# Decode attention over a key/value cache: which eight heads of a batch share a tile

## The chip, the cores and the metric

The kernel runs on one core of one Trainium2 chip. The metric is the device time of one execution in microseconds (us). Besides the times of plain runs there is one profiled execution, from which all durations are taken: its trace holds every instruction with start and duration, and every packet that the core's 16 DMA engines moved, with start, duration and bytes.

## The reference

Four decode tokens (batch 4, one position each, width 640) go through a layer norm, and then through two branches that are added to the input:

```python
x = A_x                                    # (4, 1, 640) bf16
xn = _layernorm(x)
return x + _A_ref(xn, A_k_cache, A_v_cache, A_wq, A_wo) + _B_ref(xn, B_w_in, B_w_sp, B_b_sp, B_w_out)

def _A_ref(x, k_cache, v_cache, wq, wo):   # caches: (4, 32, 4096, 128) bf16, as many q heads as kv heads
    q = (x @ wq).reshape(B, 1, 32, 128).transpose(0, 2, 1, 3)
    scores = jnp.einsum('bhqd,bhkd->bhqk', q, k_cache) * 128 ** (-0.5)
    o = jnp.einsum('bhqk,bhkd->bhqd', _softmax(scores), v_cache)
    return o.transpose(0, 2, 1, 3).reshape(B, 1, 32 * 128) @ wo
```

`_B_ref` is a small gated MLP (a gMLP with one position) over weights of 640 x 1728 and 864 x 640. The caches are the bulk: K and V have 4 x 32 heads of 4096 rows of 128 values, 1 MiB per head, 134 MB each. wq and wo have 5.2 MB each.

## The kernel before, in words

**Tiles.** The 32 heads of a batch are cut into HG = 4 groups of HT = 8 heads. A tile i is one head group hg = i // 4 of one batch b = i % 4, so there are NT = 16 tiles for K and 16 for V. In a tile a head has LN = 16 of the 128 partitions, and a partition holds NC = 256 successive cache rows of its head, 64 KB. `run_view` (L113) gives the part of the cache that makes up a tile. Since the eight heads of a group follow each other in memory, the tile is 8 MiB without a gap, seen as 128 rows of 64 KB.

**Where tiles lie.** SBUF holds one ring of UNITS = 5 units; a unit is half a tile (128 x 32 KB). K tiles take two units (`load_k`, L134), V tiles mostly two in one load, at the start and the end one unit at a time, and the very last half in four cuts (`load_v`, L141, V_CUTS L132). wq comes first, into the units that K tile 1 takes later (L104 to L106). The gMLP weights go to one unit (`load_w`, L123). wo is loaded per head group (`load_wo`, L154): three times as 128 rows of 10 KB (L157), the last time in seven parts by head (L163).

**Order of the loads.** All of them are issued on SP's queue, in the order of the list that starts at L179: K tile 0, gMLP weights, K tile 1, V tile 0, wo of group 0, K tile 2, then V and K in turn. `pump` (L203) issues the next load of the list as soon as the work that last used its units has been recorded; on the chip SP then waits for the semaphores of that work. ACT's queue carries only x, two scalars and half of the output.

**Work.** The q projection (L338 to L347) multiplies the normed x with wq, in groups of QH = 4 heads (512 columns) by 5 slices of the width; `place`, `stage_q` (L499) and `q_lanes` spread a group's q over the partitions, so that each partition has the q of its head. Then for each tile, in four quarters: VectorE multiplies K with q (L525) and mostly adds the two halves of a head's width (L541), TensorE sums the products with the identity matrix (L550), VectorE finishes the row sums (L564). The maximum and the exponentials follow (L573 to L587), ScalarE deals the probabilities out to eight masked copies (L598), TensorE multiplies them with V (L623), and `gather` (L634) collects a tile's result. A group's four tiles are normalized, turned (`group_turn`, `group_pick`) and multiplied with the group's part of wo (`group_proj`, L717), which is added into one accumulator (`out_sum`) over all groups. That sum over the groups makes it immaterial which heads a group has, as long as the q columns and the wo rows are those of its heads. The order of the instructions on TensorE, VectorE, ScalarE and SP is that of the program (L732).

Of the kernel before, what the change touches and what calls it, by code (L numbers as in the profile page):

```python
# [20 lines left out]
def kernel(  # L21
# [14 lines left out]
    nc = tc.nc  # L36
    P = nc.NUM_PARTITIONS
    Bsz, Sq, D = A_x.shape
    _, H, S, Dh = A_k_cache.shape
    HD = A_wq.shape[1]  # L40
    F = B_w_in.shape[1]
    Fh = F // 2
    DC = D // P
# [4 lines left out]
    HT = 8  # L48
    HG = H // HT
    NT = HG * Bsz  # L50
    LN = P // HT
    NC = HT * S // P
# [7 lines left out]
    CG = P // CW  # L60
# [27 lines left out]
    def units(first, n=1):  # L88
        return ring[:, first * UNIT : (first + n) * UNIT]
# [6 lines left out]
    def pair(i):  # L96
        if i in (0, NT - 1):
            return 2 if i == 0 else V_PAIR
        return 1 if i % 2 == 0 else 0
# [2 lines left out]
        return (2, 3, 0, 1) if i == 0 or (i % 2 and i < NT - 1) else (0, 1, 2, 3)  # L102

    wq_flat = ring[:, pair(1) * UNIT : pair(1) * UNIT + DC * HD]  # L104
    wq_sb = wq_flat.rearrange("p (c n) -> p c n", n=HD)
    nc.sync.dma_start(out=wq_flat, in_=A_wq.rearrange("(p c) n -> p (c n)", c=DC))  # L106

    wsp_bf = const.tile([1, 1], BF16)
# [3 lines left out]

    def run_view(cache, i):  # L113
        hg, b = divmod(i, Bsz)
        return cache[b, HT * hg : HT * (hg + 1)].rearrange("h s d -> (h s) d").rearrange(
            "(p c) d -> p (c d)", c=NC
        )

    w_sb = units(W_UNIT)
    w_in_sb = w_sb[:, 0 : DC * F].rearrange("p (c n) -> p c n", c=DC)  # L120
# [13 lines left out]
    def load_k(i):  # L134
        t = units(pair(i), 2)
        step = (1 if i == 0 else 2) * UNIT
        for e in reversed(range(0, 2 * UNIT, step)):
            nc.sync.dma_start(out=t[:, e : e + step], in_=run_view(A_k_cache, i)[:, e : e + step])
        k_tiles[i] = t.rearrange("p (c d) -> p c d", d=Dh)

    def load_v(i, part, unit, n):  # L141
        t = units(unit, n)
        cuts = V_CUTS if (i, part) == (NT - 1, 1) else (0, n * UC)
        for c0, c1 in zip(cuts, cuts[1:]):
            src = slice((part * UC + c0) * Dh, (part * UC + c1) * Dh)
            nc.sync.dma_start(out=t[:, c0 * Dh : c1 * Dh], in_=run_view(A_v_cache, i)[:, src])
        for e in range(n):
            v_tiles[i, part + e] = units(unit + e).rearrange("p (c d) -> p c d", d=Dh)

    wo_r = A_wo.rearrange("(j p r) n -> j p (r n)", p=P, r=HT)  # L150
    wo_h = A_wo.rearrange("(j h p) n -> j p h n", p=P, h=HT)
    wo_tiles = {}

    def load_wo(j):  # L154
# [15 lines left out]
    def plan_k(i):  # L170
        plan(("k", i), pair(i), 2, load_k, i)

    def plan_v(i, part, unit, n=1):
        plan(("v", i, part), unit, n, load_v, i, part, unit, n)
# [28 lines left out]
    def pump():  # L203
        while loads:
# [29 lines left out]
        out=lane_diag[:],  # L234
        in_=ident_f[:].rearrange("p (h l) -> p l h", h=HT),
# [5 lines left out]
        out=hmask[:],  # L241
        in_=ident_f[:].rearrange("p (h l) -> p h l", h=HT),
# [5 lines left out]
        out=head_scale[:].rearrange("p (h l) -> p h l", h=HT),  # L248
# [11 lines left out]
        out=sel[:],  # L260
        in_=ident_f[:].rearrange("p (g h k) -> p k h g", g=CG, k=GC),
# [5 lines left out]
        out=spread[:],  # L267
        in_=ident[:].rearrange("p (m r) -> p r m", r=HT)[:, :, None, :].to_broadcast(
            [P, HT, HT, LN]
        ),  # L270
# [3 lines left out]
        out=q_lanes[:].rearrange("r b (h l) -> r b h l", h=HT),  # L274
        in_=ident[: HT * Bsz, : HT * Bsz]
# [4 lines left out]
    QW = CW  # L280
    QH = HT // 2
# [3 lines left out]
    for g in range(CG):  # L285
        ps = slice(g * QW, (g + 1) * QW)
        for hh in range(QH):
            at_col = (g % 2 * QH + hh) * Bsz
            nc.gpsimd.tensor_copy(
                out=place[ps, hh, at_col : at_col + Bsz], in_=lane_diag[ps, 0:Bsz]  # L290
# [12 lines left out]
    for i in range(NSTAT):  # L303
# [5 lines left out]
        out=rstd[:], in_=mv[:, 1:2], func=ACT.Sqrt, bias=eps_tile[:Bsz], scale=1.0  # L309
# [4 lines left out]
        out=xn_bf[:],  # L314
# [9 lines left out]
    for c in range(DC):  # L324
        nc.tensor.transpose(  # L325
            out=xnT_ps[:, c, :], in_=xn_v[:, c, :], identity=ident[:Bsz, :Bsz]
# [8 lines left out]
    q_ps = [  # L335
        ps_m.tile([P, QH * Dh], FP32, tag="m", name="q_ps") for _ in range(NQG // CG)
    ]
    for c in range(DC):  # L338
        for hg in range(NQG):
            g = hg % CG  # L340
            nc.tensor.matmul(  # L341
                out=q_ps[hg // CG][g * QW : (g + 1) * QW, :],
                lhsT=xnT[:, c, :],
                rhs=wq_sb[:, c, hg * QH * Dh : (hg + 1) * QH * Dh],
                start=(c == 0),
                stop=(c == DC - 1),
            )  # L347
# [6 lines left out]
    def out_sum(half):  # L354
        return out_ps[OG * half : OG * half + Bsz, :]

    for half in range(2):
        nc.tensor.matmul(
            out=out_sum(half),
            lhsT=ident[:Bsz, :Bsz],  # L360
            rhs=x_bf[:, half * NOH : (half + 1) * NOH],
# [486 lines left out]
```

## Time and profile before

| | |
|---|---|
| median of 3 runs | 662.41 us (662.41 to 662.49) |
| the profiled execution | 664.69 us |
| its span, first to last instruction | 662.9 us |
| VectorE (DVE) busy | 458.5 us, 69% |
| TensorE (PE) busy | 325.6 us, 49% |
| ScalarE (ACT) busy | 82.6 us, 12% |
| GpSimd (POOL) busy | 5.6 us, 1% |
| read from memory | 282.24 MB, 426 GB/s over the span |

How to read it: the busy time of an engine is the sum of its instructions; the engines run beside each other. The DMA engines are no compute engines: there are 16 of them, and the profile gives their mean busy share, as well as packets, bytes and share of each queue. q1 is SP's queue, q10 that of ACT. In a row of waits stand the engine and line that waited, what released it, the time in total, how often, and the longest. In a table of windows a row has the stretch, the busy time and number of instructions of PE, PE's weight loads, DVE, ACT and POOL, the granted TensorE clock, the DMA share and the rate in GB/s.

The packet records show what a load is made of: one packet for each contiguous row of a partition (64 KB for a whole K or V tile, 32 KB for a unit), and packets of 4 bytes, with which the engines that share a load report that they are done.

### The profile page before, as it was taken

What the parts mean: (1) busy time and instruction counts of PE and PEld (TensorE: products, weight loads), DVE (VectorE), ACT (ScalarE), POOL (GpSimd) and SP (SyncE); (2) the same over time, 40 slices, a digit from 0 to 9 for tenths busy, and PEclk for the clock granted to TensorE, in tenths of its full rate; (3) what the DMA queues carried; (4) which work ended last, traced back from release to release, by engine and by line L of the source; (5) the groups of instructions that cost most, each with busy time, mean ns of one, the idle gap of its engine ahead of it and who ended that gap; (6) DMA issues with size and microseconds to landing.
All of it is one profiled execution on the core that took longest, in us unless ns stands there. A gap on an engine that the chain in (4) does not pass through costs nothing.

```text
span 662.9 us, 4934 instructions
## 1 busy us (share of the span) xinstructions
PE 325.6 (49%) x2131; PEld 149.9 (23%) x2131; DVE 458.5 (69%) x265; ACT 82.6 (12%) x202; POOL 5.6 (1%) x29
## 2 busy tenths in 40 slices
PE   0356462635546263463526447253563526457746
PEld 0114130212212132131212223121231212213334
DVE  2495975939488594966949397692957949488940
ACT  0103102020200202011020200202020020200200
POOL 2000000000000000000000000000000000000000
PEclk9765685778877677585867877577786857867886
DMA  9999999999999999999999999999999999999997
GB/s 378 437 398 395 423 458 435 443 429 427 428 439 440 423 443 432 404 463 423 439 436 435 428 443 424 431 439 428 435 436 435 435 435 436 416 429 437 423 429 282
DMA packets 8049, 282.56 MB, mean 426 GB/s; under 512 B 880, under 2 KB 2140, under 8 KB 2524
## 3 DMA queue, kind: packets, MB, share of 16 engines
q1 hardware_dynamic: 8008, 282.25, 99.1%
q8 instruction: 16, 0.26, 0.1%
q14 instruction: 5, 0.04, 0.0%
q10 hardware_dynamic: 20, 0.01, 0.0%
HBM read 282.24 MB, written 0.01 MB: 426 GB/s over the span
## 4 chain that ended last, share of the span: by engine, by line
DMA 62%; DVE 26%; PE 11%; issue 0%; ACT 0%; DVEq 0%; ACTq 0%
DMA ring<-in_A_k_cache_dram 57%; DVE ring L525 19%; PE s_ps L550 8%; DVE ring L541 6%; DMA ring<-in_A_v_cache_dram 3%; DMA ring<-in_A_wq_dram 2%; PE q_ps L341 1%; PE pv_acc L623 1%; PE pv L641 0%; PE out_ps L721 0%; DVE s_sb L564 0%; PE pv L653 0%; ACT pv_sb L637 0%; DVE m L573 0%; ACT res L816 0%
## 5 line engine op out<-in xcount | busy, mean ns | idle before, releaser
L550 PE MATMUL s_ps<-ring,ident 128*128 128x512 bf16 x624 | 212.8, 507 | 291.8 <-DVE ring L541 159.8
L525 DVE TENSOR_TENSOR ring<-ring,qbc 128x8192 bf16<-128x8192 bf16 x64 | 281.8, 4418 | 97.9 <-DMA ring<-in_A_k_cache_dram 97.9
L550 PEld LDWEIGHTS <-ident 128*128 128x128 bf16 x624 | 75.8, 122 | 413.2 <-issue 286.1
L541 DVE TENSOR_TENSOR ring<-ring 128x4096 bf16<-128x4096 bf16 x50 | 114.6, 2291 | 1.6
L623 PE MATMUL pv_acc<-ring,pm 128*32 128x512 bf16 x1008 | 68.7, 412 | 7.3 <-DMA ring<-in_A_v_cache_dram 7.3
L564 DVE TENSOR_REDUCE s_sb<-s_ps 128x64 f32<-128x512 f32 x64 | 43.8, 685 | 25.3 <-PE s_ps L550 25.3
L637 ACT COPY pv_sb<-pv_acc 128x512 f32<-128x512 f32 x16 | 9.4, 586 | 397.5 <-PE pv_acc L623 397.5
L598 ACT ACTIVATE pm<-p,hmask 128x256 bf16<-128x256 bf16 x120 | 49.5, 494 | 0.5
L623 PEld LDWEIGHTS <-pm 128*32 128x32 bf16 x1008 | 38.3, 143 | 38.6 <-issue 28.5
L583 DVE TENSOR_REDUCE nb<-max_ps 128x1 f32<-128x16 f32 x16 | 2.8, 174 | 37.0 <-PE max_ps L577 37.0
L641 PE MATMUL pv<-sel,pv_sb 128*128 128x8 f32 x128 | 17.8, 265 | 11.1 <-ACT pv_sb L637 11.1
L641 PEld LDWEIGHTS pv<-sel,pv_sb 128*128 128x128 f32 x128 | 16.3, 199 | 18.3 <-ACT pv_sb L637 18.3
L682 DVE TENSOR_TENSOR o_n<-pv,rden 128x32 bf16<-128x32 f32 x4 | 0.8, 192 | 15.9 <-PE pv L653 15.8
L575 ACT ACTIVATE lay<-lane_diag,m 128x16 f32<-128x16 f32 x16 | 4.9, 309 | 47.6 <-DVE m L573 47.6
L587 ACT ACTIVATE p<-s_sb,nb 128x256 bf16<-128x256 f32 x16 | 8.1, 508 | 19.5 <-DVE nb L583 19.5
L577 PE MATMUL max_ps<-lay,head_scale 128*128 128x16 f32 x32 | 6.3, 272 | 3.7 <-ACT lay L575 3.7
L511 ACT CAST q_rows<-qr_ps 32x128 bf16<-32x128 f32 x4 | 1.0, 256 | 51.8 <-PE qr_ps L503 51.8
L665 POOL TENSOR_TENSOR own_sum<-acc,hmask 128x32 f32<-128x32 f32 x4 | 2.0, 500 | 621.1 <-ACT p L587 621.1
L573 DVE TENSOR_REDUCE m<-s_sb 128x1 f32<-128x256 f32 x16 | 6.7, 420 | 0.5
L341 PE MATMUL q_ps<-ring,xnT 128*32 128x512 bf16 x40 | 4.5, 631 | 3.9 <-DMA ring<-in_A_wq_dram 3.9
L577 PEld LDWEIGHTS max_ps<-lay,head_scale 128*128 128x128 f32 x32 | 5.0, 199 | 5.6 <-ACT lay L575 5.6
L325 PE MATMUL xnT_ps<-ident,xn_bf 4*128 4x4 bf16 x5 | 0.4, 178 | 11.5 <-DVE xn_bf L313 11.5
(90 smaller groups left out, 74.6 us busy)
## 6 DMA issues: line engine op xcount, KB each, us to landing
ring<-in_A_v_cache_dram SPq DMA_DIRECT2D x7, 4096.0 KB, 23.6
ring<-in_A_k_cache_dram SPq DMA_DIRECT2D x2, 4096.0 KB, 29.2
ring<-in_A_wq_dram SPq DMA_DIRECT2D x1, 5120.0 KB
wo<-in_A_wo_dram SPq DMA_DIRECT2D x3, 1280.0 KB, 25.9
ring<-in_B_w_in_dram SPq DMA_DIRECT2D x1, 2160.0 KB, 38.4
ring<-in_A_v_cache_dram SPq DMA_DIRECT2D x1, 2048.0 KB, 20.5
ring<-in_A_v_cache_dram SPq DMA_DIRECT2D x1, 1024.0 KB, 22.2
ring<-in_A_v_cache_dram SPq DMA_DIRECT2D x2, 512.0 KB
```

What stands on the lines that cost most here:

```text
L341: nc.tensor.matmul(out=q_ps[hg // CG][g * QW : (g + 1) * QW, :], lhsT=xnT[:, c, :], rhs=wq_sb[:, c, hg * QH * Dh : (hg + 1) * QH * Dh], st ...
L525: nc.vector.tensor_tensor(out=t, in0=t, in1=qbcs[i // Bsz][:, i % Bsz, None, :].to_broadcast([P, QC, Dh]), op=ALU.mult,)
L541: nc.vector.tensor_tensor(out=t[:, :, 0:HD2], in0=t[:, :, 0:HD2], in1=t[:, :, HD2:Dh], op=ALU.add)
L550: nc.tensor.matmul(out=s[:], lhsT=ident[:], rhs=t[:, :, g * RW : (g + 1) * RW], start=(g == 0), stop=(g == n - 1),)
L564: nc.vector.tensor_reduce(out=scores[i][:, q * QC : (q + 1) * QC], in_=sums_ps.pop((i, q))[:], axis=AX.X, op=ALU.add,)
L573: nc.vector.tensor_reduce(out=m1[:], in_=scores[i][:], axis=AX.X, op=ALU.max)
L577: nc.tensor.matmul(out=ps[:], lhsT=head_scale[:], rhs=d[:], start=True, stop=True)
L587: nc.scalar.activation(out=p[:], in_=scores.pop(i)[:], func=ACT.Exp, bias=nb[:], scale=scale_qk, accum_out=acc[hg % NACC][:, b : b + 1],)
L598: nc.scalar.activation(out=p_m[i % 2][:, :, h, :], in_=probs[i][:].rearrange("p (n c) -> p n c", c=BC), func=ACT.Copy, scale=hmask[:, h : ...
L623: nc.tensor.matmul(out=pv_acc[g * CW : (g + 1) * CW, :], lhsT=pm[:, n, :, :].rearrange("p h (k c) -> p c (h k)", k=GC)[:, c, :], rhs=v_nat ...
L637: nc.scalar.copy(out=pv_sb[:], in_=pv_acc[:])
L641: nc.tensor.matmul(out=pvs[hg][:, :, b], lhsT=pv_sb[:, k * Dh : (k + 1) * Dh], rhs=sel[:, k, :], start=(k == 0), stop=stop and k == GC - 1,)
```

## The change

A tile holds every fourth head of a batch (hg, hg + 4, ..., hg + 28) instead of eight neighbouring ones. The cache is viewed as `(h j) (l c) d -> j h l (c d)`, with j the group, h the head in it and l its 16 partitions, so that a tile is now 8 pieces of 1 MiB that lie 4 MiB apart; in the built instruction the source of a K or V load is [8 heads, 16 rows, run] and the destination 128 partitions with a run each. Before, it was [128 rows, run] on both sides. The wo rows follow: three of the four wo loads have such a source of 8 x 16 rows too, while the last group's wo, in parts by head, still has 128 rows. The wq load is as before; the q projection's matmuls take their 512 columns as four runs of 128. Everything else, and the order of the instructions on every engine, is unchanged. Lines move by two.

```diff
-    wq_sb = wq_flat.rearrange("p (c n) -> p c n", n=HD)
+    wq_heads = wq_flat.rearrange("p (c h j d) -> p c j h d", c=DC, h=HT, j=HG)
...
     def run_view(cache, i):
         hg, b = divmod(i, Bsz)
-        return cache[b, HT * hg : HT * (hg + 1)].rearrange("h s d -> (h s) d").rearrange(
-            "(p c) d -> p (c d)", c=NC
-        )
+        return cache[b].rearrange("(h j) (l c) d -> j h l (c d)", j=HG, c=NC)[hg]
...
-            nc.sync.dma_start(out=t[:, e : e + step], in_=run_view(A_k_cache, i)[:, e : e + step])
+            nc.sync.dma_start(out=t[:, e : e + step], in_=run_view(A_k_cache, i)[:, :, e : e + step])
...
-            nc.sync.dma_start(out=t[:, c0 * Dh : c1 * Dh], in_=run_view(A_v_cache, i)[:, src])
+            nc.sync.dma_start(out=t[:, c0 * Dh : c1 * Dh], in_=run_view(A_v_cache, i)[:, :, src])
...
-    wo_r = A_wo.rearrange("(j p r) n -> j p (r n)", p=P, r=HT)
-    wo_h = A_wo.rearrange("(j h p) n -> j p h n", p=P, h=HT)
+    wo_r = A_wo.rearrange("(h j l r) n -> j h l (r n)", h=HT, j=HG, r=HT)
+    wo_h = A_wo.rearrange("(h j p) n -> j p h n", p=P, h=HT)
...
             nc.tensor.matmul(
-                out=q_ps[hg // CG][g * QW : (g + 1) * QW, :],
+                out=q_ps[hg // CG][g * QW : (g + 1) * QW, :].rearrange(
+                    "p (h d) -> p h d", d=Dh
+                ),
                 lhsT=xnT[:, c, :],
-                rhs=wq_sb[:, c, hg * QH * Dh : (hg + 1) * QH * Dh],
+                rhs=wq_heads[:, c, hg // 2, hg % 2 * QH : (hg % 2 + 1) * QH, :],
```

## The prediction

> **What bounds the kernel now.** I read the page's slices and DMA queues first, then the chain that ended last, then the waits of SP, which issues nearly all loads. From the page:
>
> ```profile
> DMA  9999999999999999999999999999999999999997
> ...
> DMA packets 8049, 282.56 MB, mean 426 GB/s; under 512 B 880, under 2 KB 2140, under 8 KB 2524
> ## 3 DMA queue, kind: packets, MB, share of 16 engines
> q1 hardware_dynamic: 8008, 282.25, 99.1%
> ...
> q10 hardware_dynamic: 20, 0.01, 0.0%
> ...
> DMA 62%; DVE 26%; PE 11%; issue 0%; ACT 0%; DVEq 0%; ACTq 0%
> ```
>
> All 16 DMA engines are busy 99.1% of the span. So an engine moves 282.25 MB / (0.991 x 16 x 662.9 us) = 26.9 GB/s. The trace's packet records say the same for single packets: a 64 KB row takes 2,418 ns (median of 3,456), a 32 KB row 1,213 ns (1,152 rows), 4 KB 159 ns. The 159 ns are the same when under 8 engines are moving rows of 4 KB or more as when all 16 are, so this is an engine's own pace. The windows show it too (after the clock: DMA share, GB/s):
>
> ```profile
> 300.00:400.00 100.00, 45.21 (x270) 20.15 (x271) 72.37 (x34) 10.28 (x27) 0.24 (x1) 0.74 1.00 434
> ...
> 655.00:660.00 5.00, 4.63 (x81) 2.63 (x79) 0.24 (x2) 0.00 (x0) 0.00 (x0) 0.50 0.63 226
> ```
>
> When the share falls to 0.63 the rate falls to about half and is not made up by the engines still at work. From the waits:
>
> ```profile
> DVE ring L525 <- DMA ring<-in_A_k_cache_dram: 97.9, 15, 8.1
> ...
> SPq L138 <- DVE ring L541: 256.5, 13, 21.0
> SPq L146 <- PE pv_acc L623: 146.3, 16, 12.5
> ```
>
> DVE waits for K, never K's products for DVE; SP waits for buffers, but early enough that the engines do not run dry (slices of 9). The bound is engines times an engine's pace.
>
> **The change, part by part.** Instruction counts and their order stay the same on all five engines. What is new is the shape of addresses.
>
> *The wq columns.* The 40 matmuls of the q projection (L341 before, 631 ns each) read four runs of 128 columns 1 KB apart instead of one run of 512. Bounds: nothing, to twice 40 x 631 ns = 25 us. They end at 20.6 us, while the products of the first tile wait for K, in the slower case much longer. The k(1) load waits for wq's space too, but k(0) and the gMLP weights are queued ahead of it. I take 0. Everything behind q (place, stage_q, the group steps) is untouched, and wo rows follow.
>
> *K, V and wo loads.* Before, a load's source is 128 rows of 64 KB (or part of it), one step apart. After, the built instruction carries a source of 8 heads (4 MiB apart) x 16 rows x run, against a destination of 128 partitions. Heads of a group no longer follow each other, so the two outer counts can't be merged. How a load is dealt out to engines can be counted. q1 has 54 loads and one store of 4 rows. They have 7,140 data packets; the other 868 packets of 4 bytes are 54 x 16 + 4. q10 has four small DMAs: rows 4, 1, 1 and 4, that is 10 data packets, and the other 10 of its 20 are again 4-byte packets. So a DMA has as many closing packets as engines that share it: 16 with 128 or 96 outer rows, 4 with four, 1 with one. The number follows the outer count. With an outer count of 8 on one side and 128 on the other, the shares that fit both are 8, one head and 16 partitions each. I take 8 engines. [...]
>
> The price at an undisturbed engine: 27 loads of 64 KB rows, 9 of 32 KB, one each of 16 KB (611 ns) and 8 KB (309 ns), two of 4 KB, three wo loads of 10 KB (385 ns). With 16 rows per engine and load: 432 x 2.418 + 144 x 1.213 + 16 x 0.611 + 16 x 0.309 + 32 x 0.159 + 48 x 0.385 = 1,257.5 us, against half of it, 628.8 us, on 16 engines. The other 11 loads (wq, the gMLP weights, the last wo) keep 16 engines. Check on before: 628.8 + 13.4 (wq with its slow start) + 7.8 (gMLP) + 3.6 (last wo) = 654 us, of a span of 662.9; the rest is 2.4 us for the k(1) load, whose rows take 2,714 ns, and the start and the tail. So eight undisturbed engines give 662.9 + 628.8 = 1,291.7 us of span. DVE (458.5 us busy) and PE (325.6 us) hide behind that; no load waits long for a buffer, since every load takes twice as long and the compute that frees the buffers does not.
>
> *Engines that meet.* Before, 16 engines write 128 partitions in shares that never disturb each other: 3,308 of the 3,456 packets of 64 KB take 2,418 ns. Whether shares of 16 neighbouring partitions on eight engines do is shown nowhere for long. The nearest rows are the only loads that are not 128 rows. x (L92): four engines write partitions 0 to 3 at once; packets of 1,280 bytes take 53, 53, 53 and 115 ns. The 96-row load (L129): most of its packets take 55 ns, the last ones 59 to 87, and two 7,680-byte packets beside it 415 and 458 in place of 291. These stretch 1.1 to 2.2 times, but most packets there do not stretch, and a few KB may disappear in a buffer. So the bounds are 1 and 2 times the 1,257.5 us. I take the upper end: what two engines share here, they share to the end. The first packets of k(0) start within 1.3 us of each other, 15 of 16 within 0.7 us, and from then on every engine carries the same 16 rows per load in the same order; a load is done when its slowest engine is. A brief meeting as in L129's rows becomes a lasting one.
>
> [...]
>
> The sum: 662.9 - 628.8 + 2 x 1,257.5 = 2,549 us of span. Engines that are 0.4 us apart on the way through four rows of 2.4 us save some 2% of 2,515; I take half of that, 29 us, off: 2,520. The profiled execution lay at 664.69 us, 1.8 above its span and 2.3 above the median of 662.41, which is nothing beside the other doubts: **2,520 us**.
>
> **Rivals.**
> *Eight engines, undisturbed*: rows stay at 2,418 ns. For it: the constant 2,418 ns, and the unstretched packets of L129. 662.4 + 628.8 = **1,291 us**. Chance 0.27. *In between*: the engines meet and drift apart, or one is always let through first and the other follows a few rows later; 1,350 to 2,400 us, chance 0.14.
>
> *Not slower*: the rows are still dealt out by the destination's 128 partitions, on 16 engines. The place is the dealing of each load, the price of the new addresses then nothing, and it decides if a load keeps 16 closing packets. For it: the destination is as before. Against it: the counts on q10, where both sides had the same small count, do not tell which side counts. The 2.4 us of k(1) could go with its addresses: **660 to 662.4 us**. Chance 0.08 (same 0.05, faster 0.02, slower 0.01).
>
> *The memory, not the partitions*: eight streams run 4 MiB apart in step. If the memory gives only one engine-pair's worth at a time, a row takes twice as long: also about **2,520 us**, by another mechanism. Against it: before, the partitions 64 apart already lie 64 x 64 KB = 4 MiB apart and their engines run at 2,418 ns. [...] Chance 0.06.
>
> **Chances.** Forecast 0.45. A measurement of this kernel can tell about 0.2% from no change: faster 0.02, same 0.05, slower 0.93. The range of 8 in 10 has to take in the undisturbed eight engines, whose 1,291 us could lie 20 us lower if the start and tail hide more, and the full doubling with some margin: 1,270 to 2,580 us. It leaves out the not slower case and a little above.
>
> **What the profile after would show.** Eight engines: q1 with 7,664 packets (43 loads with 8 closing packets, 11 with 16, 4 for the store: 868 becomes 524), and a share near 50% of 16 engines. Undisturbed, GB/s is near 219 and a 64 KB row takes 2,418 ns; with engines that meet, near 112 and 4,836 ns. With 8,008 packets and 99%, the dealing was not changed, and I am wrong from the first step. If the share is near 50% but the rows lie between, the engines drift. DVE's and PE's busy times should stay at about 458 and 326 us (a lower granted clock could move PE's); idle time at L525 behind K should grow to most of the span, and SP's waits for DVE and PE should nearly vanish.

## The result and the profile after

The changed kernel takes 2,505.82 us (median of 6 runs, 2,437.17 to 2,575.0); the kernel before, on the same chip, 662.47 us (6 runs, 662.41 to 662.77). The ratio is 3.695, 95% interval 3.676 to 3.7145; it rests on the two shortest of the six runs alone, which is why it lies below the ratio of the medians, and the profiled execution (2,562.95 us, span 2,561.2) is one of the longer runs. What may make the runs differ so much is taken up below.

The slices, queues and engines of the page after:

```profile
PE 355.0 (14%) x2131; PEld 160.7 (6%) x2131; DVE 458.7 (18%) x265; ACT 82.6 (3%) x202; POOL 5.6 (0%) x29
...
PEclk6555555555655555556555555555655555565555
DMA  7545544545545555444455545554455444544354
GB/s 183 120 106 119 123 113 113 112 112 113 112 108 112 111 114 120 119 106 99 102 106 106 106 100 106 110 107 105 100 107 106 104 106 102 109 107 105 85 110 113
DMA packets 7705, 282.55 MB, mean 110 GB/s; under 512 B 536, under 2 KB 1796, under 8 KB 2180
...
q1 hardware_dynamic: 7664, 282.24, 49.7%
```

The bytes are the same, 282.24 MB. Two things changed. The share of 16 engines fell from 99.1% to 49.7%, which is the time of eight engines without a gap. And the rate fell not to half but to a quarter: 110 GB/s on eight engines is 14 GB/s for each, against 26.9 before. The packet records say how: 8,008 packets became 7,664, because the closing packets of 4 bytes went from 868 to 524, and a 64 KB row now takes 4,931 ns in the median instead of 2,418 ns (3,456 rows both times, mean 4,816 against 2,432).

The instruction counts and the busy time of DVE are those of before; PE is busy a tenth longer under a granted clock of 0.553 instead of 0.727. The waits:

```profile
DVE ring L525 <- DMA ring<-in_A_k_cache_dram: 1120.4, 17, 83.2
...
PE pv_acc L623 <- DMA ring<-in_A_v_cache_dram: 913.3, 20, 80.1
...
DVE s_sb L564 <- PE s_ps L550: 769.8, 17, 59.4
```

Both caches are waited for now. The third row is V's too: in the order of TensorE's instructions some sums stand behind a block of V's products, and in the trace they come after it, and VectorE waits for the sums: at 378 to 436 us TensorE stands 57.5 us before V's products, the sums follow at 439.0, and VectorE goes on at 441.0 after 58.3 us. The chain that ended last shows a limit of the view:

```profile
another core or an unknown queue 78%; DVE 12%; PE 9%; DMA 1%; issue 1%; ACT 0%; DVEq 0%; ACTq 0%
```

There is no other core. The page's list of issues gives no time to landing for any K or V load any more, so the chain has nothing to put these waits down to. The rows of waits above name the loads, and the queue's share agrees.

### The profile page after: what moved, and what is told of

It is laid out like the page before. It is cut to its first block, busy times and chain, and to the rows that moved or that the text cites. A ratio compares the mean times of both kernels' runs of the same rounds, so it can differ in the third digit from the quotient of the medians.

```text
span 2561.2 us, 4934 instructions
## 1 busy us (share of the span) xinstructions
PE 355.0 (14%) x2131; PEld 160.7 (6%) x2131; DVE 458.7 (18%) x265; ACT 82.6 (3%) x202; POOL 5.6 (0%) x29
## 3 DMA queue, kind: packets, MB, share of 16 engines
q1 hardware_dynamic: 7664, 282.24, 49.7%
HBM read 282.24 MB, written 0.01 MB: 110 GB/s over the span
## 4 chain that ended last, share of the span: by engine, by line
another core or an unknown queue 78%; DVE 12%; PE 9%; DMA 1%; issue 1%; ACT 0%; DVEq 0%; ACTq 0%
DVE ring L525 8%; PE s_ps L550 4%; PE pv_acc L623 4%; DVE ring L541 3%; PE pv L641 1%; DMA ring<-in_A_wq_dram 1%; DVE s_sb L564 1%; ACT pv_sb L637 0%; PE out_ps L721 0%; PE max_ps L577 0%; PE q_ps L339 0%; DVE nb L583 0%; PE pv L653 0%; DVE m L573 0%
## 5 line engine op out<-in xcount | busy, mean ns | idle before, releaser
L525 DVE TENSOR_TENSOR ring<-ring,qbc 128x8192 bf16<-128x8192 bf16 x64 | 281.9, 4419 | 1120.4 <-DMA ring<-in_A_k_cache_dram 1120.4
L623 PE MATMUL pv_acc<-ring,pm 128*32 128x512 bf16 x1008 | 93.5, 534 | 913.3 <-DMA ring<-in_A_v_cache_dram 913.3
L623 PEld LDWEIGHTS <-pm 128*32 128x32 bf16 x1008 | 47.0, 151 | 956.1 <-issue 951.0
L587 ACT ACTIVATE p<-s_sb,nb 128x256 bf16<-128x256 f32 x16 | 8.1, 507 | 49.7 <-DVE nb L583 49.7
```

The costliest lines, as they stand in the source:

```text
L525: nc.vector.tensor_tensor(out=t, in0=t, in1=qbcs[i // Bsz][:, i % Bsz, None, :].to_broadcast([P, QC, Dh]), op=ALU.mult,)
L587: nc.scalar.activation(out=p[:], in_=scores.pop(i)[:], func=ACT.Exp, bias=nb[:], scale=scale_qk, accum_out=acc[hg % NACC][:, b : b + 1],)
L623: nc.tensor.matmul(out=pv_acc[g * CW : (g + 1) * CW, :], lhsT=pm[:, n, :, :].rearrange("p h (k c) -> p c (h k)", k=GC)[:, c, :], rhs=v_nat ...
```

## The experiments

Three theories. *Partitions*: a load whose source has two outer counts, 8 x 16, is shared by eight engines, each with 16 neighbouring partitions, and engines whose partitions lie 32 apart take turns at one entry of SBUF. An entry is here a name for what four neighbouring partitions and the four that lie 32 further would share; that they share anything is the assumption that the runs test. The packet records do not say which engine wrote a row, so the partitions of an engine, and which engines take a load of few rows, are inferred throughout. *Memory*: eight streams 4 MiB apart collide in memory. *Dealing*: a load with two outer counts runs its engines at half pace in itself. All three give about 2,500 us for the changed kernel.

**Other addresses, same shares.** In the kernel before:

```diff
-        return cache[b, HT * hg : HT * (hg + 1)].rearrange("h s d -> (h s) d").rearrange(
-            "(p c) d -> p (c d)", c=NC
-        )
+        rows = cache.rearrange("b h (l c) d -> (b h l) (c d)", c=NC)
+        return rows[127 * i : 127 * i + 136].rearrange("(h l) e -> h l e", l=17)[:, 0:LN]
```

> The kernel before, but a K or V load's source is 8 pieces of 16 rows that lie 17 rows (1 MiB and 64 KB) apart, so that it keeps two outer counts and 8 shares; the destination is as in the changed kernel. The tiles hold other cache rows than the reference asks for, and the pieces are no heads. wo and q are as before. Theory 'partitions' (engines whose partitions lie 32 apart take turns at one entry of SBUF): the addresses do not matter, 64 KB rows near 4,900 ns, 2,380 to 2,530 us. Theory 'memory' (eight streams 4 MiB apart in step collide): the pitch is odd now, rows back at 2,418 ns, about 1,280 us. Theory 'dealing' (any load with two outer counts runs its engines at half pace): also 2,400 to 2,530 us.

2,541.84 us, still on half of the engines:

```profile
q1 hardware_dynamic: 7688, 282.24, 50.7%
```

64 KB rows take 4,967 ns in the median. So it is not the pitch of 4 MiB: 1 MiB and 64 KB is no better.

**Other addresses, shares of before.** In the kernel before, in place of the same three lines:

```diff
+        return cache.rearrange("b h (l c) d -> (b h) l (c d)", c=NC)[:, i]
```

> The kernel before, but a tile holds one 64 KB row of each of the 128 heads of all batches: one outer count of 128 with a step of 1 MiB, 16 engines, each with its partitions of before. [...] The tiles hold other cache rows than the reference asks for. Theory 'partitions': nothing collides, 655 to 670 us. Theory 'memory': rows take about twice 2,418 ns, near 1,300 us or more. Theory 'dealing': 655 to 670 us.

682.59 us. The queue and the rate:

```profile
DMA packets 8049, 282.56 MB, mean 415 GB/s; under 512 B 880, under 2 KB 2140, under 8 KB 2524
...
q1 hardware_dynamic: 8008, 282.25, 98.7%
```

All 16 engines are back at nearly full pace, with rows 1 MiB apart; the median row is 2,418 ns and one in nine is over 2,700 (one in 28 before). So such addresses cost about 20 us here, a bit above the range that the partitions theory gave (655 to 670), and nothing near a doubling.

**Eight engines that do not meet.** In the kernel before, four loads of 32 partitions in place of one of 128 (K's are shown, V's are cut in the same way):

```diff
+        rows = cache.rearrange("b h (l c) d -> (b h l) (c d)", c=NC)
+        return rows[125 * i : 125 * i + 160].rearrange("(g h l) e -> g h l e", g=4, l=5)[:, :, 0:4]
...
+            for g in range(4):
+                nc.sync.dma_start(
+                    out=t[32 * g : 32 * (g + 1), e : e + step],
+                    in_=run_view(A_k_cache, i)[g][:, :, e : e + step],
+                )
```

> The kernel before, but each K or V load is made as four loads of 32 partitions, with a source of 8 pieces of 4 rows (5 rows apart): still two outer counts and 8 engines, but an engine has four partitions of its own, in all four loads the same ones modulo 32. The tiles hold other cache rows than the reference asks for. Theory 'partitions': no two engines meet, 64 KB rows at 2,418 ns, 662.4 + 628.8 less the three wo loads that stay on 16 engines, about 1,270 to 1,300 us. Theory 'dealing': rows stay near 4,900 ns, 2,400 to 2,530 us. Theory 'memory': pitch is odd, about 1,280 us.

1,290.59 us:

```profile
GB/s 299 209 218 227 217 226 214 212 224 214 214 222 214 216 239 218 218 214 222 216 214 222 216 214 239 216 216 218 218 216 216 218 218 214 220 218 212 216 217 185
...
q1 hardware_dynamic: 8648, 282.25, 51.6%
```

Still half of the engines (51.6%), still two outer counts, but 64 KB rows are back at 2,418 ns. Dealing in itself costs no pace. The prediction's 1,291 us for eight undisturbed engines is this run. It and the run of 2,541.84 us both have eight engines and an odd pitch; what differs is that a load covers 32 partitions with four for each engine, instead of 128 with 16 neighbouring ones for each. That is worth a factor of 2.0 between these two, and the 1.9 that remains to the changed kernel.

**Sixteen engines, two views.** First the changed kernel with rows outermost:

```diff
-        return cache[b].rearrange("(h j) (l c) d -> j h l (c d)", j=HG, c=NC)[hg]
+        return cache[b].rearrange("(h j) (l c) d -> j l h (c d)", j=HG, c=NC)[hg]
```

> The changed kernel, but partitions are dealt as row by head instead of head by row: source of 16 rows (64 KB apart) x 8 heads (4 MiB apart), so that 16 engines share a load, each with 8 neighbouring partitions; the rows of q and the masks are not moved along, so heads meet wrong queries. Theory 'partitions': engines 0 and 4, 1 and 5 and so on lie 32 partitions apart and meet in pairs, rows of 64 KB near 4,800 ns on 16 engines, 1,240 to 1,310 us. Theory 'memory': the rows that run at one time lie 64 KB apart as before, only an engine's own next row is 4 MiB on, 660 to 690 us. A theory that only the number of engines counts: 660 to 690 us (the three wo loads stay on eight).

1,369.64 us, with the engines busy all the time and slow:

```profile
DMA packets 8025, 282.56 MB, mean 207 GB/s; under 512 B 856, under 2 KB 2116, under 8 KB 2500
...
q1 hardware_dynamic: 7984, 282.24, 98.6%
```

64 KB rows take 5,080 ns. The number of engines alone does not decide, and a share that reads 99% busy may be half of it waiting. It is above the range, 1,240 to 1,310 us, for two reasons. A shared row is 2.1 and not 2 times an undisturbed one: the rows of K and V fill 1,297 us of an engine, where twice 619.6 were expected (628.8 less the wo loads). And the three wo loads, whose 10 KB rows take 1,020 ns in the median, fill 53 us of their eight engines, where 48 rows of 2 x 385 ns would be 37.

The 128 rows of the kernel before are dealt to 16 engines too, eight rows each, and run at 2,418 ns. So they can't be dealt as neighbouring eights like these; how they are, no record here says.

Then two loads of 64 partitions in the kernel before, with 16 pieces of 4 rows, cut as in the run with eight engines (`g=2`, 64 partitions in place of `g=4`, 32):

> The kernel before, but each K or V load is made as two loads of 64 partitions with a source of 16 pieces of 4 rows (5 rows apart): 16 engines, each with four partitions; engine e and engine e + 8 lie 32 partitions apart. The tiles hold other cache rows than the reference asks for. The run with eight engines that each had four partitions of their own took 1,290.59 us with rows at 2,418 ns. Theory 'partitions', blocks 32 apart share an entry: twice the engines bring nothing, rows at 4,836 to 5,130 ns, 1,280 to 1,380 us, and no drift in time can help. If only overlapping or neighbouring shares disturb each other: rows at 2,418 ns, 655 to 690 us.

1,327.58 us, rows 5,065 ns:

```profile
DMA packets 8690, 282.57 MB, mean 213 GB/s; under 512 B 1520, under 2 KB 2780, under 8 KB 3164
...
q1 hardware_dynamic: 8648, 282.25, 99.5%
```

This is the run with eight engines of four partitions, doubled: every block of four partitions still has one engine, no two shares overlap, and the second eight engines bring nothing. So here the pace is set by something that partitions 0 to 31 share with 32 to 63, and one engine for each block of four uses it up: 2 x 65,536 bytes in 5,065 ns are 25.9 GB/s, against 27.1 for one engine alone (65,536 bytes in 2,418 ns).

**One load for each head**, 16 rows to 16 partitions, in the changed kernel (K's loads; V's likewise):

```diff
+            for h in range(HT):
+                nc.sync.dma_start(
+                    out=t[LN * h : LN * (h + 1), e : e + step],
+                    in_=run_view(A_k_cache, i)[h, :, e : e + step],
+                )
```

> The changed kernel with its output as the reference has it, but each K or V load is made as eight loads, one for each head: 16 rows to 16 partitions, one outer count of 16, so 16 engines take one partition each. Theory 'partitions': four engines meet in each block of four partitions, 64 KB rows take about 4 x 2,418 = 9,670 ns, the total stays that of four entries, 2,400 to 2,560 us. If engines drift apart over the heads, less, 1,300 to 2,400 us. A theory that only the number of engines counts: 660 to 700 us.

2,415.48 us, rows 9,160 ns, 3.8 times the undisturbed ones, with all 16 engines busy:

```profile
DMA packets 12509, 282.61 MB, mean 117 GB/s; under 512 B 5336, under 2 KB 6596, under 8 KB 6980
...
q1 hardware_dynamic: 12464, 282.26, 98.4%
```

Four engines for each block of four partitions: if the four always stand there together, 4 x 65,536 bytes in 9,160 ns are 28.6 GB/s for a block. Sixteen engines on 16 partitions bring 117 GB/s, about four times one engine's 27.1, where 16 engines on 128 partitions brought 426.

This run also answers a wider memory theory, that the rows read at one time lie badly, whatever their pitch. Here and in the run with rows outermost, each of the 16 engines reads one row of the same head and then goes on to the same next head: as long as they keep in step, the same addresses in the same order. Rows take 5,080 ns there and 9,160 ns here. What differs is the partitions they go to, and that there are eight loads in place of one; four in place of one left the rows at 2,418 ns in the run of 1,290.59 us.

**q and wo alone.** K and V as before, the q columns and wo rows as after.

> The changed kernel with K and V loaded as before, 128 rows of neighbouring heads; only the q columns and the wo rows follow the new head groups, so that heads meet queries and wo rows of others. By the prediction: the q matmuls cost 0; three wo loads on eight engines that meet cost 3 x (16 x 2 x 0.385 - 8 x 0.385) = 27.7 us, 690 us. If the wo loads' engines do not meet (16 rows of 10 KB are short): 3 x 8 x 0.385 = 9.2 us, 671.6 us. If the eight free engines run ahead into the next tile meanwhile: 662 to 670 us.

697.91 us (696.79 to 698.81), ratio to before 1.0534, interval 1.051 to 1.0558. The wo loads' 10 KB rows take 768 ns in the median, not 385: they do meet. The window with the first of these loads (60 to 100 us), and one without any:

```profile
60.00:100.00 40.00, 21.34 (x130) 8.99 (x126) 31.44 (x25) 9.29 (x23) 0.00 (x0) 0.63 1.00 325
100.00:250.00 150.00, 63.90 (x384) 28.46 (x385) 98.06 (x46) 16.36 (x42) 0.24 (x1) 0.72 1.00 429
```

It is 8 us more than the 690 expected. In the three stretches in which wo's rows run (81 to 97, 290 to 305, 458 to 472 us) rows of K and V stretch as well, up to 6.8 us: the eight engines without wo go on to the next tile, and likely write at the same entries. That these stretched rows make up the 8 us is likely, not shown.

**Engines out of step.** Does it matter that two engines pass the same partitions at the same time? The changed kernel with a wq load that holds some engines back:

```diff
-    nc.sync.dma_start(out=wq_flat, in_=A_wq.rearrange("(p c) n -> p (c n)", c=DC))
+    wq_src = A_wq.rearrange("(p c) n -> p (c n)", c=DC)
+    at = 0
+    for n in [2] * 10 + [6] * 10 + [48]:
+        nc.sync.dma_start(out=wq_flat[at : at + n, :], in_=wq_src[at : at + n, :])
+        at += n
```

> The changed kernel with its output as the reference has it; only the first load, wq, is cut differently: ten loads of 2 rows, ten of 6 and one of 48 in place of one of 128, so that engines 0 and 1 have 23 rows of 40 KB, engines 2 to 5 have 13 and the others 3. Engines 0 and 1 then run 15 us behind 2 and 3, and 4 and 5 behind 6 and 7; four rows of 64 KB take an undisturbed engine 9.7 us. Theory 'partitions' with engines in step: the pairs no longer stand at the same four partitions, rows go back to 2,418 ns: 1,291 us and some 25 us for the late start, 1,300 to 1,400 us, as long as the shift lasts. If loads that wait for buffers bring the engines back into step: 1,400 to 2,450 us. A theory in which eight shares of 16 partitions are slow whatever the others do at the time: 2,440 to 2,600 us.

2,347.45 us (2,270.31 to 2,424.41). From the rows of SP:

```profile
SPq L109 <- DMA ring<-in_A_wq_dram: 35.0, 10, 5.2
...
0.73 50.46 SPq L109 DMA_DIRECT2D ring<-in_A_wq_dram  x21
54.43 5.32 SPq L140 DMA_DIRECT2D ring<-in_A_k_cache_dram  x2
```

Not what was meant: the 21 loads waited for each other, and SP issued the last of them, 48 rows for all 16 engines, only at 51 us. K tile 0 followed at 54 us, when all 16 engines were moving these 48 rows, three each (the DMA share from 54 to 58 us is 1.09); they were not idle, as the next expectation has it, but the uneven loads lay behind them and nothing held some engines back any more. The four runs all lie below the six of the changed kernel, and 3% of the 64 KB rows take under 2,700 ns (0.2% there); whether some shift was left, the run does not tell. Once more with few loads, where the first gMLP weight comes in pieces:

```diff
-    nc.sync.dma_start(out=wq_flat, in_=A_wq.rearrange("(p c) n -> p (c n)", c=DC))
+    wq_src = A_wq.rearrange("(p c) n -> p (c n)", c=DC)
+    nc.sync.dma_start(out=wq_flat[0:102, :], in_=wq_src[0:102, :])
+    nc.sync.dma_start(out=wq_flat[102:P, :], in_=wq_src[102:P, :])
...
+    W_CUTS = ((0, 34), (34, 114), (114, P))
...
+    load_w_in(*W_CUTS[0])
```

> The changed kernel with its output as the reference has it; wq comes as two loads (102 rows on engines 0 to 5, 17 each, then 26), and 34 rows of the first gMLP weight come ahead of K tile 0 as a load of its own, 17 rows for each of engines 0 and 1; its other rows follow as 80 and 14. No load of K tile 0 waits for any of these, so that engines 4 and 5 reach it 25.7 us behind 6 and 7, and 0 and 1 10.9 us behind 2 and 3 (in the first attempt SP issued K tile 0 only when all engines were idle). Theory 'partitions' with engines in step: the pairs stand at different blocks of four partitions, rows of K and V near 2,418 ns as long as the shift lasts, 1,310 to 1,500 us; if waits for buffers take the shift away, rows near 2,418 ns at first and near 4,900 ns later, 1,500 to 2,400 us. A theory in which a share of 16 partitions is slow whatever the others do: rows near 4,900 ns from the start, 2,440 to 2,600 us.

Four runs took 1,437.24, 2,077.82, 2,343.91 and 2,348.78 us. Two windows of the profiled one (2,077.82), and after them an early one of the changed kernel:

```profile
50.00:200.00 150.00, 39.76 (x239) 17.06 (x240) 61.48 (x44) 10.19 (x20) 0.00 (x0) 0.57 0.51 178
1200.00:1500.00 300.00, 46.57 (x262) 20.33 (x261) 64.57 (x33) 9.38 (x24) 0.00 (x0) 0.56 0.50 117
...
50.00:150.00 100.00, 20.85 (x134) 9.99 (x134) 32.86 (x32) 7.49 (x16) 0.00 (x0) 0.52 0.52 119
```

Same share of the engines, but 178 GB/s early and 117 later, where the changed kernel has 119 from the start. Of the 64 KB rows that start in the first 300 us 63% take under 2,700 ns, of those from 300 to 1,500 us 5%. So shares of 16 partitions are not slow as such; that they are slow while two engines stand at the same entry fits this. The shift was lost on the way in the profiled run and, going by the times alone, in two others; the fourth, 1,437.24 us, seems to have kept it for most of the way, but was not profiled. What takes it away was not separated: a wait for buffers could, since an engine that is ahead then runs out of work, but no run shows that this is it.

## Why the prediction was right

**Eight engines.** Right to the packet: 7,664 in q1, 524 of them closing packets, as counted. The counts ahead of it were for 128, 96, 4 and 1 rows, so eight for 8 x 16 was an estimate. The traces now show 8 closing packets for each load of 8 x 16 against 128, and 16 for 16 x 8 (7,984 packets, 844 closing: 16 for every load but the three of wo). Other counts fit in sum, not load by load: with the loads that stay as they were, the two runs that cut wq come to their 604 and 543 closing packets if 2, 6 and 48 rows go to 2, 6 and 16 engines in the one, and 102, 26, 34, 80 and 14 rows to 6, 13, 2, 16 and 14 in the other.

**Engines that meet.** Right in the end taken, twice an undisturbed row. No row before showed it for long, so this was a choice between two bounds, and the forecast had a chance of 0.45. No run before showed which engines would meet either. The experiments put it in the partitions: not the addresses (2,541.84 us with others), not the dealing (1,290.59 us with partitions of one's own), but partitions 32 apart. The runs with 4 and 8 partitions for each of 16 engines (rows of 5,065 and 5,080 ns) and with 16 for each of eight (4,931 ns) fit this set of partners, at 25.9 GB/s for an entry with two engines (5,065 ns) and up to 28.6 with four (9,160 ns). The step in the argument that a meeting lasts because the engines stay in step has the shifted run for it: 63% of the rows took under 2,700 ns in the 300 us after some engines had been held back.

**The size.** 2,520 against 2,505.82 us. The terms are less exact than the sum. A shared row takes more than 4,836 ns when its engines stay together, 5,049 ns in the median from 1,150 to 2,250 us of the profiled execution. In that stretch the closing packets of a load stayed close, for example two at 1,795.5 and 1,798.5 us and six at 1,808.3 to 1,810.8 (which engine sent which is not recorded). From 250 to 1,150 us the mean was 4,631 ns (4,966 in the later stretch), 4% under 4,836 where I took off 1%, which fits engines that are partly apart. Over the whole execution the mean is 4,816 ns: the two errors cancel, and that the sum comes within 1% of the median is luck as far as this goes. The four rows at one entry from which the 29 us were worked out are shown by no run; what the rows show in place of that 1% is this mean, 0.4% under 4,836. The runs themselves spread from 2,437 to 2,575 us; that engines are apart by more in one run than in another would fit, but only one execution has a trace.

**The wo loads.** Mis-sized a little: 35.5 us (697.91 - 662.43) in place of 27.7, with the rows at 768 ns where 2 x 385 put them.

**The q columns at 0.** The 40 matmuls take 631 ns in the median against 634 before, so the four runs of 128 columns cost nothing here.

**SP's waits.** Wrong. I expected them nearly to vanish, because every load takes longer and the compute does not:

```profile
SPq L136 <- DVE ring L541: 1038.9, 13, 96.9
SPq L144 <- DMA ring<-in_A_v_cache_dram: 924.6, 15, 90.5
```

SP waits for VectorE to release a K tile, and VectorE can't start before that tile has landed: a wait for compute holds the load's time in it. The second row names a load of V itself. It cost nothing, as the eight engines had work all the time (49.7% of 16). Idle time at L525 also grew less than I wrote, to 1,120 of 2,561 us, because V's part of the waiting appears on TensorE and behind it.

**The rivals.** Eight undisturbed engines would have been right had the shares been four partitions wide (1,290.59 us); the memory rival fell with the odd pitch (2,541.84 us); and nothing kept the 16 engines. In between, 1,350 to 2,400 us, did not come out for this kernel, whose lowest run is 2,437 us, but the four runs with some engines held back lie there (1,437 to 2,349 us), which fits engines that move apart or together on the way, as that rival had it. Rows 1 MiB apart took 682.59 us, 3% more, and the eight streams with a pitch of 1 MiB and 64 KB were no faster than those 4 MiB apart (2,541.84 us).

## What to carry to other kernels

Read a load's source as the dealing sees it: in the loads here the number of engines went with the outermost counts of the two sides (16 closing packets for 128 rows and for 16 x 8, 8 for 8 x 16 against 128), not with the length of a row (128 rows of 4 KB and of 64 KB both had 16), and the closing packets in the queue's count tell the number before and after. Then ask which partitions each engine gets: two engines that stood at blocks of four partitions 32 apart at the same time shared one engine's pace (25.9 GB/s), so a share of 98.6% was half as fast (207 GB/s), and a view that cannot be merged into one run of 128 rows cost 3.7 times here though no byte was added. In a kernel bound by loads like these, one outer count of 128 was fast even with rows 1 MiB apart (682.59 us). Where the pieces don't allow it, taking them off the outside (16 engines, 1,369.64 us) or giving each of eight engines a block of four of its own (1,290.59 us) saves about half of what the changed kernel takes.

## What the runs showed that I had not expected

A program on one core whose six runs beside it lay at 662.41 to 662.77 us became one that varies by over 5% (2,437 to 2,575 us) by the same work, and with some engines held back at the start by over 60% (1,437 to 2,349 us). And two engines at one entry do a little worse than one alone (25.9 against 27.1 GB/s). For four the rows give 28.6, but only if all four are always at the same block; engines that are a head ahead would give that number too, and no run separates the two.
